# Nineteen small loads into unused columns, between the last weight loads of a decode layer

## The chip, the cores and the metric

The kernel runs on one core of one Trainium2 chip. A core has engines that run their own instruction streams: TensorE (PE, with its weight loads as PEld), VectorE (DVE), ScalarE (ACT), GpSimd (POOL) and SyncE (SP). They wait for each other by semaphores. Sixteen DMA engines move data between HBM and the on-chip memory (SBUF), and SP, ACT and POOL can issue loads to them. The metric is the device time of one execution in microseconds (us), lower is better.

## The reference

One decode step of a transformer layer with adaptive layer norm: four sequences (B = 4), one token each, width 512.

```
mod = (silu(c) @ w_mod) split in six: sa, ca, ga, sb, cb, gb
h = layernorm(x) * (1 + ca) + sa
x = x + ga * attention(h)      # 32 query heads on 8 kv heads of 128, the last 2048 cached positions, then @ wo
h = layernorm(x) * (1 + cb) + sb
x = x + gb * ((silu(h @ w1) * (h @ w3)) @ w2)     # w1, w3: 512 x 1792, w2: 1792 x 512
```

Everything is float32. The weights and the cached keys and values are about 101 MB, and each is read once.

## The kernel before

All large inputs come through one SBUF buffer, `ring`, of 6 x 8192 float32 columns on 128 partitions, cut into three slots of 16384 columns. A slot holds one group's keys and values (8 MB) or weights. The loads are issued by SP in the order in which they are needed (only wq goes through ACT): w_mod_a, the key and value blocks of seven groups, wo_mod (a half of wo and the rest of w_mod), the last group's keys with more of wo, its values, the rest of wo, then w1, w3 and w2. A load is issued as soon as the last reader of the columns that it overwrites is done, so SP waits for PE most of the time, and the loads stand in line at the DMA engines for some 40 us.

`Program` records each operation with the tiles that it reads and writes, adds the waits that overlaps ask for, and emits the operations engine by engine in the order of the code. Every recorded operation is emitted by one line, L57. A load that anyone waits for has a semaphore of its own. `do.mark()` cuts the program in two parts: the first part's semaphores are cleared by GpSimd (L136) once PE, DVE, ACT and SP have all passed the mark, which PE does just before its products with the last piece of w2.

Around the change stand these steps. `project_out(3)` multiplies with the last part of wo_mod that lies in columns 6144 to 8191 of slot 0; `mod_columns` reads columns 8192 to 16383 of it. Then `group(G - 1, [4, 5])` is the attention of the last group. The load of w3 goes to the upper half of slot 0, and the load of w2 to the first 7168 columns of the lower half, in four pieces of 7, 4, 2 and 1 blocks of 512 columns (`W2_CUTS`), so that the products with w2 can begin before all of it is there. Columns 7168 to 8191 of slot 0 are used by nothing after `project_out(3)`. After the attention come the second norm, the products with w1 (gate), with w3 (up), the product of both into `hidT`, and the products with w2: the first 7 blocks into `part`, the other 7 into `y_ps`. Two DVE operations and one store of 32 KB end the program.

Of the kernel before, what the change touches and what calls it, by code (L numbers as in the profile page):

```python
# [8 lines left out]
B, D, HQ, G, SK, DH, W, FF = 4, 512, 32, 8, 8192, 128, 2048, 1792  # L9
# [5 lines left out]
NF = len(CHUNKS)  # L15
W2_CUTS = [0, 7, 11, 13, 14]
EPS = 1e-5
HALF = 8192
# [127 lines left out]
def block_kernel(nc, w_mod_a, wq, kv_in, wo_mod, last_k_wo, last_v, wo, w1, w3, w2, out):  # L146
# [5 lines left out]
    do = Program(nc)  # L152
# [8 lines left out]
    slots = [ring[:, n * 2 * HALF : (n + 1) * 2 * HALF] for n in range(3)]  # L161
# [10 lines left out]
    def load(dst, src, cuts=(0, 1), queue="sync"):  # L172
        step = src.shape[1] // cuts[-1]
        for lo, hi in zip(cuts[:-1], cuts[1:]):
            do(queue, "dma_start", dst[:, lo * step : hi * step], src[:, lo * step : hi * step])
        return dst[:, : src.shape[1]]
# [114 lines left out]
    for half in range(2):  # L291
        qp = s_ps[half]
        for k in range(4):
            for i in range(4):
                at = ((half * 4 + i) * 4 + k) * 512
# [26 lines left out]
    def heads_out(g):  # L322

        otp = bank()[:, : R * B]
        if g < G - 1:
            do("tensor", "matmul", otp, o_sum, pick, start=True, stop=True)
        else:
            for c in range(NC):
                do("tensor", "matmul", otp, work[:, c * P : (c + 1) * P], pick_c[:, c].rearrange("p r b -> p (r b)"), start=(c == 0), stop=(c == NC - 1))
        do("vector", "tensor_copy", oT[:, g].rearrange("p r b -> p (r b)"), otp)  # L330
# [60 lines left out]
    do("vector", "tensor_scalar_add", cb1, cb1, 1.0)  # L391
    group(G - 1, [4, 5])
    w3_t = load(slots[0][:, HALF:], w3)
    w2_t = load(slots[0][:, :HALF], w2, W2_CUTS)
    heads_out(G - 1)
    project_out(G - 2)
# [118 lines left out]
```

## Time and profile before

| what | value |
|---|---|
| median of 3 runs | 242.45 us (242.39 to 242.96) |
| span of the profiled execution, first to last instruction | 241.1 us |
| busy share of PE, DVE, ACT, POOL | 61%, 23%, 10%, 1% |
| moved by the DMA engines | 101.38 MB, 421 GB/s on average |
| w1, w3 and the four pieces of w2 issued by SP | at 181.64, 192.84, 193.21, 193.68, 194.18 and 194.67 us |
| store of the result issued | at 239.56 us |

The profiled execution's span is 1.35 us shorter than the median time of the runs. The profile gives each group of instructions as engine, line, operation, output<-input, shape, count and times; "SPq" is SP's own queue, and "us to landing" counts from the issue of a load to the last of its completion signals. In the strip of 40 digits each digit is the busy share of the 16 DMA engines in one fortieth of the window, in tenths.

### The profile page before, as it was taken

Reading aid. Unit: us, or ns where it says so; the run is one execution under the profiler, and the core shown is the slowest. Engines: PE = TensorE matmul, PEld = TensorE weight load, DVE = VectorE, ACT = ScalarE, POOL = GpSimd, SP = SyncE. Lnnn points to the kernel's source line nnn. Section 1 sums busy time; section 2 is a strip of 40 time slices with the busy share of each in tenths; the row PEclk is TensorE's granted clock in tenths of the full one; section 3 lists DMA queues with packets and bytes.
Section 4 is the critical chain, followed back from the end, with each engine's and each line's share of the span. In section 5 each row is a group of like instructions: output and inputs, shape, how many; then the busy total and the mean of one; then the engine's idle time right before and its main releaser. Section 6 shows DMA issues by size and latency. Waiting matters only on the chain.

```text
span 241.1 us, 2468 instructions
## 1 busy us (share of the span) xinstructions
PE 146.8 (61%) x1103; PEld 52.8 (22%) x1103; DVE 55.2 (23%) x140; ACT 24.0 (10%) x36; POOL 2.6 (1%) x11
## 2 busy tenths in 40 slices
PE   0000169756782972945767586567296919964876
PEld 0000132213222312201311222221131202422333
DVE  4000220240303124123132124130312014103120
ACT  2000000103003003001200300300300000320100
POOL 3000000000000000000000000000000000000000
PEclk9999997995977799779797589797977997996899
DMA  8999989898989898989999999999999999999993
GB/s 316 414 436 425 500 370 500 351 511 359 511 359 503 370 502 370 489 383 478 391 479 391 478 394 468 402 468 405 457 413 424 435 405 435 407 432 426 416 415 133
DMA packets 2889, 101.38 MB, mean 421 GB/s; under 512 B 448, under 2 KB 448, under 8 KB 704
## 3 DMA queue, kind: packets, MB, share of 16 engines
q1 hardware_dynamic: 2736, 92.85, 89.5%
q10 hardware_dynamic: 144, 8.39, 8.1%
q8 instruction: 8, 0.13, 0.2%
q14 instruction: 1, 0.01, 0.0%
HBM read 101.20 MB, written 0.03 MB: 420 GB/s over the span
## 4 chain that ended last, share of the span: by engine, by line
DMA 73%; PE 20%; DVE 3%; ACT 2%; issue 0%; SPq 0%
DMA ring<-kv_in 30%; DMA ring<-wo_mod 17%; DMA ring<-w 15%; DMA ring<-w_mod_a 11%; PE s_ps L57 8%; PE bank L57 7%; PE o_ps L57 4%; PE a_ps L57 2%; ACT p_sb L57 2%; DVE nm L57 2%; DVE p_sb L57 0%; DVE e L57 0%; DVE sq L57 0%; DVE xc L57 0%; DVE tot L57 0%
## 5 line engine op out<-in xcount | busy, mean ns | idle before, releaser
L57 PE MATMUL s_ps<-ring,qT 128*32 128x512 f32 x256 | 37.0, 731 | 20.2 <-DMA ring<-kv_in 14.7
L57 PE MATMUL bank<-ident,p_sb 128*128 128x128 f32 (+1 forms) x136 | 27.4, 350 | 30.8 <-ACT p_sb L57 30.7
L57 PE MATMUL o_ps<-ring,pT 128*16 128x512 f32 x256 | 37.8, 696 | 0.0
L57 PEld LDWEIGHTS bank<-ident,p_sb 128*128 128x128 f32 (+1 forms) x136 | 19.6, 177 | 51.9 <-ACT p_sb L57 31.7
L57 ACT ACTIVATE p_sb<-s_ps,nm 128x2048 f32<-128x2048 f32 (+1 forms) x11 | 16.5, 1501 | 143.2 <-DVE oT L57 105.2
L57 DVE TENSOR_REDUCE nm<-s_ps 128x1 f32<-128x2048 f32 x7 | 16.0, 2292 | 34.5 <-PE s_ps L57 34.5
L57 DVE COPY pT<-bank 128x64 f32<-128x64 f32 x32 | 7.2, 224 | 56.1 <-PE bank L57 56.1
L57 PEld LDWEIGHTS s_ps<-ring,qT 128*32 128x32 f32 x256 | 9.0, 131 | 47.5 <-issue 20.7
L57 PE MATMUL bank<-ident,xs 128*128 128x128 f32 x1 | 0.5, 473 | 27.8 <-POOL xs L57 27.8
L57 PE MATMUL s_ps<-ring,h2T 128*32 128x512 f32 (+1 forms) x64 | 9.1, 664 | 2.3 <-DMA ring<-w 2.3
L57 PE MATMUL a_ps<-ring,oT 128*4 128x512 f32 x64 | 9.1, 709 | 2.0 <-DMA ring<-wo_mod 2.0
L57 PE MATMUL s_ps<-ring,hT 128*32 128x512 f32 x64 | 8.8, 711 | 0.4 <-DVE hT L57 0.4
L57 PEld LDWEIGHTS o_ps<-ring,pT 128*16 128x16 f32 x256 | 5.4, 98 | 11.6 <-issue 9.2
L57 DVE SCALAR_TENSOR_TENSOR o_own<-o_ps,rl,own 128x512 f32<-128x512 f32 x7 | 5.3, 751 | 11.1 <-PE o_ps L57 11.1
L57 DVE TENSOR_REDUCE o_sum<-o_own 128x128 f32<-128x512 f32 x7 | 7.2, 1029 | 0.2
L57 PE MATMUL bank<-ring,sc 128*32 128x256 f32 (+1 forms) x64 | 7.2, 610 | 0.0
L57 PEld LDWEIGHTS bank<-ident,xs 128*128 128x128 f32 x1 | 0.2, 180 | 27.8 <-POOL xs L57 27.8
L57 DVE TENSOR_SCALAR e<-e 128x16 f32<-128x16 f32 x1 | 0.2, 174 | 23.8 <-ACT e L57 23.8
L57 DVE TENSOR_REDUCE mx<-s_ps 128x1 f32<-128x512 f32 x4 | 2.8, 691 | 7.6 <-PE s_ps L57 7.6
L57 DVE COPY qT<-bank 128x64 f32<-128x64 f32 x8 | 2.2, 277 | 9.8 <-PE bank L57 9.4
L57 PEld LDWEIGHTS s_ps<-ring,h2T 128*32 128x32 f32 x64 | 2.6, 129 | 7.4 <-issue 4.5
L57 PE MATMUL s_ps<-ring,hidT 128*32 128x64 f32 (+1 forms) x126 | 3.7, 262 | 0.3 <-DVE hidT L57 0.3
(93 smaller groups left out, 55.4 us busy)
## 6 DMA issues: line engine op xcount, KB each, us to landing
ring<-w SPq DMA_DIRECT2D x2, 3584.0 KB, 38.3
ring<-last_k_wo SPq DMA_DIRECT2D x1, 6144.0 KB, 30.5
ring<-last_v SPq DMA_DIRECT2D x1, 4096.0 KB, 39.9
ring<-w_mod_a SPq DMA_DIRECT2D x1, 2064.0 KB, 26.6
ring<-wo SPq DMA_DIRECT2D x1, 2048.0 KB, 43.4
ring<-w SPq DMA_DIRECT2D x1, 1792.0 KB, 40.9
ring<-w SPq DMA_DIRECT2D x1, 1024.0 KB, 42.9
ring<-w SPq DMA_DIRECT2D x1, 512.0 KB, 43.7
```

The source lines that it names most:

```text
L57: op = Op(engine, lambda: getattr(getattr(self.nc, engine), method)(*args, **kw), [])
```

## The change

Between the load of w3 and the load of w2 twenty operations are added; nothing is removed. Fifteen are loads by SP: load n (1 to 15) takes n rows of 4n columns, 16n bytes a row, out of w3, and writes them to the same rows of the unused columns. Four are loads by GpSimd of 2, 8, 3 and 8 rows of 2048, 2064, 2080 and 2096 bytes, out of w3 too. The last is a GpSimd memset of all 1024 unused columns on 128 partitions, which waits for all nineteen loads. Nothing reads these columns.

```
     w3_t = load(slots[0][:, HALF:], w3)
+    spare = slots[0][:, NF * D : HALF]
+    for n in range(1, 16):
+        at = 2 * n * (n - 1)
+        do("sync", "dma_start", spare[:n, at : at + 4 * n], w3[:n, at : at + 4 * n])
+    for lo, hi, step, m in ((32, 34, 1, 512), (0, 32, 4, 516), (40, 43, 1, 520), (64, 96, 4, 524)):
+        do("gpsimd", "dma_start", spare[lo:hi:step, 480 : 480 + m], w3[lo:hi:step, 480 : 480 + m])
+    do("gpsimd", "memset", spare, 0.0)
     w2_t = load(slots[0][:, :HALF], w2, W2_CUTS)
```

The order of instructions changes on two engines. On SP, between wo and the end, this stood before (`w` stands for w1, w3 and w2; the shape is rows x columns, and `x2` are w1 and w3):

```order
L57 DMA ring<-wo 128x4096
L57 DMA ring<-w 128x7168 x2
L57 DMA ring<-w 128x3584
L57 DMA ring<-w 128x2048
L57 DMA ring<-w 128x1024
L57 DMA ring<-w 128x512
L57 DMA out<-p_sb 128x64
```

and this stands there now, from the twelfth small load on:

```order
L57 DMA ring<-w 12x48
L57 DMA ring<-w 13x52
L57 DMA ring<-w 14x56
L57 DMA ring<-w 15x60
L57 DMA ring<-w 128x3584
L57 DMA ring<-w 128x2048
L57 DMA ring<-w 128x1024
L57 DMA ring<-w 128x512
```

The four pieces of w2 have moved behind fifteen more issues on SP; none of the fifteen has a wait of its own, since the wait of w3 already covers it.

On POOL, which had nothing between the copy of x near the start and the clearing of the semaphores (`L136 ISA`), the difference is this:

```order
 L57 MEMSET xs 128x128
 L57 COPY xs<-ring 128x16
+L57 DMA ring<-w 2x512
+L57 DMA ring<-w 8x516
+L57 DMA ring<-w 3x520
+L57 DMA ring<-w 8x524
+L57 MEMSET ring 128x1024
 L136 ISA
```

The first of the four loads waits for PE (the last product of `project_out(3)`), the memset for nineteen loads, and the clearing now stands behind both. PE, DVE and ACT keep their instructions in the same order.

## The prediction

> **What bounds the kernel.** I read the page's head and its strip of DMA shares first, then the chain that ended last.
>
> ```profile
> span 241.1 us, 2468 instructions
> DMA  8999989898989898989999999999999999999993
> DMA packets 2889, 101.38 MB, mean 421 GB/s; under 512 B 448, under 2 KB 448, under 8 KB 704
> q8 instruction: 8, 0.13, 0.2%
> DMA 73%; PE 20%; DVE 3%; ACT 2%; issue 0%; SPq 0%
> ```
>
> The sixteen DMA engines are at 80 to 90% and more in every slice but the last, and 73% of the chain is waiting for loads. The kernel is bound by bytes; the end is set by the last ones, and the chain's last pieces show how:
>
> ```profile
> 192.84 37.00 DMA ring<-w
> 229.84 0.04 issue
> 229.88 3.71 PE s_ps L57 x20
> ...
> 234.91 0.27 DVE hidT L57
> 235.18 0.04 issue
> 235.22 3.80 PE s_ps L57 x138
> 239.02 0.02 issue
> 239.05 0.23 DVE p_sb L57
> ```
>
> The load of w3, issued at 192.84, lands at 229.84; hidT is ready at 235.18; then PE multiplies with w2 until 239.02. The chain books those 3.80 us to PE, so I looked at whether PE waits for w2 inside them. The issues of the four pieces, one row each of SP's timeline, their landings in the same order (KB each, us from issue to landing), and the stored result:
>
> ```profile
> 193.21 0.43 SPq L57 DMA_DIRECT2D ring<-w  x1
> 193.68 0.45 SPq L57 DMA_DIRECT2D ring<-w  x1
> 194.18 0.45 SPq L57 DMA_DIRECT2D ring<-w  x1
> 194.67 0.44 SPq L57 DMA_DIRECT2D ring<-w  x1
> ...
> ring<-w SPq DMA_DIRECT2D x1, 1792.0 KB, 40.9
> ring<-w SPq DMA_DIRECT2D x1, 1024.0 KB, 42.9
> ring<-w SPq DMA_DIRECT2D x1, 512.0 KB, 43.7
> ring<-w SPq DMA_DIRECT2D x1, 256.0 KB, 43.8
> out<-p_sb SPq DMA_DIRECT2D x1, 32.0 KB, 1.5
> ...
> 236.66 0.16 PEld L57 LDWEIGHTS s_ps<-ring,hidT 128*32 128x32 f32 x5 [0.43 <-DMA ring<-w]
> ```
>
> Sums: the pieces land at 234.1, 236.6, 237.9 and 238.5. The first is there 1.1 us before hidT asks for it. The second is waited for: PE's weight loads stand 0.43 us and go on at 236.66. The fourth lands 0.5 us before PE is done. So a delay of the last three pieces by d moves the end by d; a delay of the first by less than 1.1 us costs nothing by itself.
>
> The engines do not finish together, which decides who may be delayed. Busy time and DMA share (the last two columns are share and GB/s) in three stretches of the end, and the two queues in the window 230 to 238.6:
>
> ```profile
> 230.00:236.40 6.40, 5.86 (x51) 2.31 (x52) 0.91 (x3) 0.58 (x1) 0.00 (x0) 1.00 0.96 399
> 236.40:237.90 1.50, 1.50 (x74) 1.09 (x72) 0.00 (x0) 0.59 (x1) 0.00 (x0) 1.00 0.50 190
> 237.90:238.60 0.70, 0.70 (x62) 0.70 (x56) 0.00 (x0) 0.00 (x0) 0.00 (x0) 1.00 0.01 3
> ...
> q1 hardware_dynamic: 517, 2.82, 79.5%
> q8 instruction: 1, 0.02, 0.8%
> ```
>
> From 236.4 to 237.9 half of the engine time is used: about eight engines have finished, and eight carry on for some 1.5 us. A cause is in the second queue: one instruction fetch packet costs 0.8% of 16 engines x 8.6 us = 1.1 us on the one engine that it falls on, and the page counts eight of them. Which engines are the late ones no view says.
>
> **The change, part by part.**
>
> *Fifteen loads by SP: their issue.* SP's rows above stand 0.47 to 0.50 us apart, so fifteen more take 15 x 0.49 = 7.4 us, and w2's pieces are issued from 200.6 to 202.1. Cover: the engines are on w1 and w3 until w3 lands at 229.84, so there are about 27 us to spare, and an issue would have to take over 2 us each before the engines run dry. No row of SP shows a dearer issue than 0.45 us; I cost it at nothing.
>
> *Their packets.* They lie in the queue after w3 and before w2, hence they delay all four pieces of w2 and not w3. For the price I take the store, 128 rows of 256 bytes, in the window 240.3 to 240.8:
>
> ```profile
> DMA packets 144, 0.03 MB, mean 66 GB/s; under 512 B 144, under 2 KB 144, under 8 KB 144
> q1 hardware_dynamic: 144, 0.03, 31.1%
> ```
>
> 144 packets are 128 rows and 16 completions, one for each engine. They took 31.1% of 16 x 0.5 us = 2.49 us, or 17 ns each. The fifteen loads have 1 + 2 + ... + 15 = 120 rows of 16 to 240 bytes. The large loads spread eight rows to an engine; a load of n rows can use at most n engines. If the rows start from the same engine each time, the first engine gets one row and one completion of each load, 30 packets x 17 ns = 0.52 us, and the last gets none. Spread evenly it would be at most (120 + 240)/16 = 22.5 packets = 0.39 us; all rows on one engine, 135 packets = 2.3 us. I take 0.52, since a row to an engine is what the large loads show, and because the end goes by the latest engine.
>
> The Trainium skill, in "DMA: Bandwidth & Descriptors", section "Why a DMA increments its semaphore by 16 and not by 1", says that a load from SP uses the largest number of engines up to 16 that divides its outer size, and then the lowest-numbered ones. By that, n rows go to engines 0 to n-1, and the sum is the same 0.52 us on engine 0. No load in the trace of before has fewer than 128 rows, so no row bears on it.
>
> *What a load costs beside its packets, in a queue that is full.* The trace has 512 KB in 237.9 - 236.6 = 1.3 us and 256 KB in 238.5 - 237.9 = 0.6 us: half the bytes, half the time, so a further load costs between nothing and about 0.1 us (the landings are given to 0.1). For fifteen that is 0 to 1.5 us. I take 0, which the 1024 KB in 2.5 us support, and keep 1.5 for the range.
>
> The Trainium skill's same page, section "Anatomy of one DMA — SWDGE (gpsimd) path", gives a fixed part of about 2.0 us a DMA, and its "Rules for kernel authors" call a transfer under 64 KB mostly overhead. Nineteen in a row would be 38 us by it, an estimate. The pieces of w2 disagree as long as other loads are in line, with 0.6 us for 256 KB.
>
> *Four loads by GpSimd.* They wait for the last of `project_out(3)`; the products ran here:
>
> ```profile
> 183.60 5.31 PE L57 MATMUL a_ps<-ring,oT 128*4 128x512 f32 x32 [1.99 <-DMA ring<-wo_mod]
> 2.01 0.95 POOL L57 MEMSET qT<- 128x1024 f32 x1
> 27.50 0.21 POOL L57 COPY xs<-ring 128x16 f32<-128x16 f32 x1 [24.39 <-DMA ring<-w_mod_a]
> 233.62 0.43 DVE L57 COPY p_sb<-s_ps 32x256 f32<-32x256 f32 x1 [4.05 <-PE s_ps L57]
> ```
>
> So they are issued from 188.9 on, by a POOL that has been idle since 27.7. Before has no issue by POOL; SP's 0.45 is the nearest row, and with 28 us until w2's turn several us each would still be hidden. Their bytes come on top of a full queue wherever they land: 21 rows of 2 KB. w2's fourth piece has 8 such rows on each engine in 0.6 us, or 0.08 each. An engine gets one or two rows (21/16 = 1.3), 0.16, and up to four completions, 4 x 17 ns = 0.07: 0.23 us. On one engine alone it would be 21 x 0.08 = 1.7 us; nothing at all if they fall on early engines.
>
> *The memset.* It waits for the fifteen loads behind w3, so it starts about 230.5 and takes the 0.95 us of qT's row, of the same shape; nineteen waits may add 1 us. DVE stands idle for 4.05 us before 233.62, PE does not wait for POOL, and ring's columns there are read by nobody. Behind it on POOL is only the clearing, which PE's mark lets go shortly before 238.5: 6 us of cover. Without it the end would wait for POOL from about 241 on. Nothing.
>
> *Sum.* 0.52 + 0.23 = 0.75 us on the latest engine, if it is among those that take the most small rows. The span goes from 241.1 to 241.85. The median of the runs is 1.35 us above that span, and I leave this as it is: 242.45 + 0.75 = 243.2.
>
> **The rivals.**
>
> *Hidden by the early engines.* If the engines with most of the small rows are among the eight that finish 1.5 us early, they have room for 0.75 us. The late ones then bear, say, seven loads of the fifteen (14 x 17 ns = 0.24) and the GpSimd part (0 to 0.23): 0.25 to 0.5 us, 242.7 to 242.95. For it: the stretch with half of the engines done. Against it: eight of sixteen are late, so that all of the first few are early is the smaller part, and rows this short may cost more than the store's 17 ns. It ends inside 0.3% (0.73 us, up to 243.18), which is about what a measurement of this kernel can tell from no change.
>
> *One engine takes whole loads.* Were all rows of a small load on one engine, and that the same one, 135 packets x 17 ns = 2.3 us there; with GpSimd's 0.23 that gives 245.0, or 243.5 if the engine is an early one with 1.5 us of room. It decides from 0.75 us on the last engine. Against it: the large loads are spread.
>
> *Every small load makes its own round trip.* The store needs 1.5 us from issue to landing. If an engine finished each small load before it turned to the next, 15 x 1.5 = 22 us would stand between w3 and w2: 265. Against it: w2's 0.6 us for 256 KB.
>
> *A gain.* Were the instruction fetches shifted to other engines by the added traffic, the late half could end up to half of 1.5 us sooner: 242.45 - 0.75 = 241.7. Nothing in the change points there; it only could.
>
> **How the numbers follow.** Forecast (0.73 to 1.9 us more, the sum with the fixed part of up to 0.1 a load partly real): 0.45. Hidden or nearly: 0.42. One engine with whole loads: 0.07. Round trips, or a POOL so slow that it sets the end: 0.03. A gain over 0.3%: 0.03. Slower is 0.45 + 0.07 + 0.03 = 0.55, within 0.3% 0.42, faster 0.03. For the range I leave out the lower part of the hidden case, under 242.5 (about 0.05, with the 0.03 of a gain), and above 244.7 (0.75 + 1.5 from the unknown fixed part) most of the whole-load case and the round trips, about 0.1. The forecast's own range is 243.2 to 244.3.
>
> **What would show it.** In the profile of after: w2's pieces issued 7.4 us later with w3 landing within 0.3 us of 229.84; the four pieces landing later by the same 0.5 to 0.9 us each and PE's wait before the second piece longer by that; hidT no later than 0.3 us; the memset done by 233; the 1.5 us stretch with half of the engines still there. If w2's landings stay within 0.3 us, the early engines have hidden it; a first piece later than 1.1 us and with a gap of DMA share after 229.8 would mean round trips; landings later by 2 us with only one engine busy, whole loads on one engine. The prediction is wrong outright if SP's issues take over 2 us each, if w3 itself moves by over 0.5 us, or if the time outside the span changes because of loads from GpSimd.

## The result, and the profile after

The changed kernel takes 243.75 us (median of 4 runs, 243.72 to 243.83) where the kernel before takes 242.45: 1.3 us more, ratio 1.005 with a 95% interval of 1.0034 to 1.0066. The forecast was 0.75 us more (243.2) within 242.5 to 244.7. The profiled execution grew by the same amount, from 241.1 to 242.4, so the time lies inside the span. The page of after, from its head, its DMA queues and its chain:

```profile
span 242.4 us, 2497 instructions
DMA packets 3257, 101.44 MB, mean 419 GB/s; under 512 B 795, under 2 KB 795, under 8 KB 1072
q1 hardware_dynamic: 2976, 92.87, 89.5%
q0 software_dynamic: 128, 0.04, 0.1%
DMA 74%; PE 17%; DVE 3%; SPq 2%; ACT 2%; issue 1%
```

Bytes and the share of the main queue are as before; 240 packets are new on q1 (120 rows and 120 completions) and 128 on q0, the queue of GpSimd's loads. The last pieces of the chain that ended last, and the weight loads of PE that wait:

```profile
196.98 0.39 SPq L57
197.37 0.04 issue
197.41 40.51 DMA ring<-w
237.92 0.04 issue
237.96 2.34 PE s_ps L57 x128
240.30 0.02 issue
240.32 0.23 DVE p_sb L57
...
237.96 0.94 PEld L57 LDWEIGHTS s_ps<-ring,hidT 128*32 128x32 f32 x64 [1.40 <-DMA ring<-w]
```

Before, the chain went through hidT and booked the end to PE; now it names the second piece of w2, and PE's wait for it has grown from 0.43 to 1.40 us. The issues of w2's pieces in SP's timeline, and their landings (KB each, us from issue):

```profile
196.98 0.39 SPq L57 DMA_DIRECT2D ring<-w  x1
197.41 2.26 SPq L57 DMA_DIRECT2D ring<-w  x1
199.72 6.11 SPq L57 DMA_DIRECT2D ring<-w  x1
205.87 6.46 SPq L57 DMA_DIRECT2D ring<-w  x1
...
ring<-w SPq DMA_DIRECT2D x1, 1792.0 KB, 38.4
ring<-w SPq DMA_DIRECT2D x1, 1024.0 KB, 40.5
ring<-w SPq DMA_DIRECT2D x1, 512.0 KB, 39.4
ring<-w SPq DMA_DIRECT2D x1, 256.0 KB, 33.9
```

Sums: 235.4, 237.9, 239.1 and 239.8, against 234.1, 236.6, 237.9 and 238.5. All four pieces are 1.2 to 1.3 us later, while w3 (issued at 191.27, 38.8 us to landing) came at 230.1 instead of 229.8. So about 0.2 us arise ahead of w3's landing (the completions show them already at w1's, 221.51 against 221.32) and 1.1 between it and w2's first piece. Two stretches of the end (the last two columns are DMA share and GB/s) show that the engines are still out of step, but that fewer are done early:

```profile
230.00:236.40 6.40, 5.64 (x48) 2.35 (x51) 1.63 (x6) 0.58 (x1) 0.95 (x1) 1.00 0.98 397
236.40:237.90 1.50, 1.08 (x10) 0.15 (x3) 0.00 (x0) 0.38 (x1) 0.00 (x0) 1.00 0.83 336
```

The share from 236.4 to 237.9 rose from 0.50 to 0.83. The rest is as forecast: POOL's four issues and its memset are out of everybody's way:

```profile
187.69 2.18 POOL L57 DMA_DIRECT2D ring<-w  x4 [159.94 <-PE bank L57]
231.93 0.95 POOL L57 MEMSET ring<- 128x1024 f32 x1 [42.06 <-DMA ring<-w]
233.82 0.43 DVE L57 COPY p_sb<-s_ps 32x256 f32<-32x256 f32 x1 [3.03 <-PE s_ps L57]
235.11 0.25 DVE L57 TENSOR_TENSOR hidT<-eg,bank 128x56 f32<-128x56 f32 x1 [0.55 <-PE bank L57]
```

hidT is ready at 235.36, as w2's first piece lands: of the 1.1 us between the two nothing is left.

The completion signals recorded in the trace tell more than the views. Here are those of four small loads of the changed kernel (us; one value for each engine that reports, in order of time):

```
rows  completions
  1   192.12  228.61
  2   192.46  228.54 228.79
  5   193.41  228.45 228.92 229.07 229.33 229.63
  6   193.74  228.65 229.10 229.25 229.51 229.82 230.04
w3 (16 engines)          228.27 to 228.52 on eight, 229.26 to 230.04 on eight
w2, first piece          232.66 to 235.42
```

A load of n rows has one early signal at its issue and n later ones: n engines, one row on each. That is what the Trainium skill states in "DMA: Bandwidth & Descriptors", section "Why a DMA increments its semaphore by 16 and not by 1" (the lowest-numbered engines up to the largest divisor, the issuer writes the rest at once), and the trace agrees in both (it counts the engines and shows the same ones coming back, but does not number them). The engine that serves the one-row load reports at 228.61, then 228.79, and so on: 0.17 to 0.2 us from one small load to the next, although the packets were worked out at 17 ns each. The engine that the six-row load adds comes last, at 230.04, because it is one of the eight late ones.

### The profile page after: what moved, and what is told of

Same layout as the page of the kernel before. It is cut to its first block, busy times and chain, and to the rows that moved or that the text cites. A ratio compares the mean times of both kernels' runs of the same rounds, so it can differ in the third digit from the quotient of the medians.

```text
span 242.4 us, 2497 instructions
## 1 busy us (share of the span) xinstructions
PE 150.1 (62%) x1103; PEld 53.4 (22%) x1103; DVE 55.2 (23%) x140; ACT 24.0 (10%) x36; POOL 5.8 (2%) x16
## 4 chain that ended last, share of the span: by engine, by line
DMA 74%; PE 17%; DVE 3%; SPq 2%; ACT 2%; issue 1%
DMA ring<-kv_in 31%; DMA ring<-w 17%; DMA ring<-wo_mod 16%; DMA ring<-w_mod_a 11%; PE bank L57 7%; PE s_ps L57 5%; PE o_ps L57 4%; SPq L57 2%; DVE nm L57 2%; ACT p_sb L57 2%; PE a_ps L57 1%; DVE p_sb L57 0%; DVE e L57 0%; DVE sq L57 0%; DVE xc L57 0%
## 5 line engine op out<-in xcount | busy, mean ns | idle before, releaser
L57 PE MATMUL s_ps<-ring,qT 128*32 128x512 f32 x256 | 37.7, 743 | 19.6 <-DMA ring<-kv_in 12.4
L57 PE MATMUL bank<-ident,p_sb 128*128 128x128 f32 (+1 forms) x136 | 28.7, 361 | 30.8 <-ACT p_sb L57 30.7
L57 PE MATMUL o_ps<-ring,pT 128*16 128x512 f32 x256 | 38.7, 711 | 0.0
L57 PEld LDWEIGHTS bank<-ident,p_sb 128*128 128x128 f32 (+1 forms) x136 | 20.7, 184 | 52.8 <-ACT p_sb L57 31.7
L57 PE MATMUL s_ps<-ring,h2T 128*32 128x512 f32 (+1 forms) x64 | 9.7, 701 | 0.9 <-DMA ring<-w 0.6
L57 PE MATMUL s_ps<-ring,hT 128*32 128x512 f32 x64 | 9.8, 783 | 0.4 <-DVE hT L57 0.4
L57 PE MATMUL a_ps<-ring,oT 128*4 128x512 f32 x64 | 7.4, 592 | 1.1 <-DMA ring<-wo_mod 1.1
L57 POOL DMA_DIRECT2D ring<-w x4 | 2.2, 552 | 159.9 <-PE bank L57 159.9
## 6 DMA issues: line engine op xcount, KB each, us to landing
ring<-w SPq DMA_DIRECT2D x2, 3584.0 KB, 38.8
```

The costliest lines, as they stand in the source:

```text
L57: op = Op(engine, lambda: getattr(getattr(self.nc, engine), method)(*args, **kw), [])
```

## The experiments

Two theories stood against each other at the start, with a third for GpSimd's loads. **A, packets** (the prediction's): a small load costs an engine its row and its completion, 2 x 17 ns. **B, a price for each load**: 0.13 us on every engine that it uses, whatever it carries. The figure of B is from after: the late engine that takes ten of the fifteen loads (six rows and up) ends them at 231.88 and w2's first piece at 235.42; it ended w3 at about 229.8, so the first piece was due 4.3 us later, at 234.1, and is 1.3 us late (4.3 us is what lies between the two in the kernel before, 229.84 to 234.1). Each kernel was timed in turn with the kernel before, which ran at 242.42 to 242.49 us. The first two cuts of code below show what is gone against the changed kernel, the others what stands in place of the nineteen loads; the lines that set `spare` and the loops over n are in part left out, and the memset stays in every kernel that has small loads.

### The fifteen alone, and the four alone

```
-    for lo, hi, step, m in ((32, 34, 1, 512), ...):
-        do("gpsimd", "dma_start", spare[lo:hi:step, ...], ...)
```

> The fifteen loads of 1 to 15 rows by SP and the memset, without the four loads by GpSimd. Theory A (packets: 17 ns for each row and each completion, the prediction's): at most 0.52 us later than before, w2's last piece lands by 239.0. Theory B (each small load costs every engine that it uses about 0.13 us, whatever its rows carry): the latest engine takes ten or more of them, +1.1 to +1.3 us, w2's last piece lands at 239.6 to 239.8. Theory C (the GpSimd loads make the difference): 0 to +0.3 us.

Measured: 243.27 us against 242.42, ratio 1.004 (1.0027 to 1.0053), +0.85 us.

```
-    for n in range(1, 16):
-        at = 2 * n * (n - 1)
-        do("sync", "dma_start", spare[:n, at : at + 4 * n], w3[:n, at : at + 4 * n])
```

> The four loads by GpSimd and the memset, without the fifteen by SP. Theory A: up to +0.23 us. Theory B: 0 to +0.3 us, the landing of w3 later by that and the pieces of w2 unchanged behind it. Theory C: +1.0 us or more.

Measured: 242.59 us against 242.42, ratio 1.0008 (0.9999 to 1.0017), +0.17 us, which the interval does not tell from nothing. C is out: the time comes from SP's fifteen loads. They cost more than A's 0.52: the interval is 0.65 to 1.28 us, and B's lower end, 1.1, lies in it. w2's last piece landed at 239.4, later than A's 239.0 and earlier than B's 239.6 to 239.8. The two parts sum to 1.0 of the 1.3 us; the 0.3 left is inside the intervals.

### One engine alone: 24 loads of one row, 15 loads of three rows

```
+    for n in range(24):
+        do("sync", "dma_start", spare[:1, 40 * n : 40 * n + 32], w3[:1, 40 * n : 40 * n + 32])
```

> Instead of the nineteen loads, twenty-four loads by SP of one row of 128 bytes each, and the memset; all on one engine, one of those that finish w3 about 1.6 us before the last. Theory A: 48 packets x 17 ns = 0.8 us, less than the engine's room: no change. Theory B: 24 x 0.13 = 3.1 us on that engine, less 1.6 of room: +1.3 to +1.7 us, with one engine's landings of w2 alone behind the others'.

Measured: 244.09 us against 242.42, ratio 1.0072 (1.006 to 1.0085), +1.67 us. A, which expected no change, is out, and by 24 rows that are 3 KB together. The pieces of w2 in this kernel:

```profile
207.91 30.41 DMA ring<-w
...
ring<-w SPq DMA_DIRECT2D x1, 1792.0 KB, 29.1
236.40:237.90 1.50, 1.50 (x14) 0.30 (x6) 0.00 (x0) 0.00 (x0) 0.00 (x0) 1.00 0.52 206
```

Of the sixteen completions of the first piece fifteen come from 232.17 to 234.10 as before, and one at 235.86. That engine ended w3 early, at about 228.0, so its first piece was due 4.3 us later, at 232.3. It is 3.56 us late, 0.15 for each load.

The counterpart puts a like burden on early engines without exceeding their room:

```
+        do("sync", "dma_start", spare[:3, at : at + 4 * n], w3[:3, at : at + 4 * n])
```

> Instead of the nineteen loads, fifteen loads by SP of 3 rows each, and the memset: the three lowest engines take 15 of them, and in the run with 1 to 15 rows these three were among the eight that finish w3 about 1.5 us early. Theory A: 30 x 17 ns = 0.5 us, hidden: no change. Theory B: 15 x 0.13 to 0.15 = 2.0 to 2.2 us, less the room of 1.5 to 1.6: +0.3 to +0.7 us, with three engines' landings of w2 behind the others'.

Measured: 242.67 us against 242.49, ratio 1.0007 (0.9998 to 1.0016): not told from no change. This is below what B expected, but the trace shows the mechanism B names. The stretch of the end in this kernel:

```profile
236.40:237.90 1.50, 1.50 (x66) 0.82 (x62) 0.00 (x0) 0.53 (x1) 0.00 (x0) 1.00 0.70 279
```

The DMA share in it is 0.70, not 0.50: 3 of 16 engines more are busy (0.50 + 3/16 = 0.69). Five engines end the first piece before 233.0 where eight did. The three delayed ones have merged with the late half. The room of the early engines is real, and it swallowed 15 loads on each of three engines.

### All engines alike: 16 rows, then rows of 2 KB

```
+        do("sync", "dma_start", spare[:16, at : at + 4 * n], w3[:16, at : at + 4 * n])
```

> Instead of the nineteen loads, fifteen loads by SP of 16 rows each (16 to 240 bytes a row), and the memset: every engine gets one row of every load, the late ones too. Theory A: 30 packets x 17 ns = +0.52 us. Theory B: 15 x 0.13 = +1.95 us on all engines alike.

Measured: 245.0 us against 242.42, ratio 1.0102 (1.0089 to 1.0116), +2.58 us. w3 landed at 193.03 + 36.9 = 229.9 and the first piece of w2 at 236.2:

```profile
193.03 0.33 SPq L57 DMA_DIRECT2D ring<-w  x1
ring<-w SPq DMA_DIRECT2D x1, 3584.0 KB, 36.9
...
200.34 35.85 DMA ring<-w
236.20 0.14 issue
236.33 5.37 PE s_ps L57 x135
...
236.20:239.70 3.50, 3.37 (x18) 1.03 (x20) 0.00 (x0) 0.00 (x0) 0.00 (x0) 0.51 0.78 318
239.70:241.70 2.00, 1.96 (x129) 1.80 (x123) 0.00 (x0) 0.59 (x1) 0.00 (x0) 1.00 0.07 23
```

Of 6.25 us between the two, 4.3 are usual: 1.95 us for fifteen loads, 0.13 each, as B said to the tenth. The other 0.5 us is not in the loads. The first piece now comes after hidT is ready, PE starts late, and in this execution the granted clock was 0.51 from 236.2 to 239.7 (the column before the DMA share), where it was 1.0 at that place in the kernel before. PE ends 1.1 us after w2's last landing instead of 0.5. The kernel with rows of 2 KB, next, speaks for the clock and against the late first piece as the cause: there the piece comes later still, the granted clock is 1.0 from 237.8 to 241.4, and the end moves by no more than w2's landings (3.7 us). The clock was not changed by itself. The first piece's cover of 1.1 us, which the prediction named, is overdrawn here; in the changed kernel it was used up to the last tenth.

The same with 512 columns a row asks whether the 0.13 us runs beside a transfer:

```
+        p, at = n // 2 * 16, n % 2 * 512
+        do("sync", "dma_start", spare[p : p + 16, at : at + 512], w3[p : p + 16, at : at + 512])
```

> As the fifteen loads of 16 rows, but with rows of 2048 bytes: every engine gets 15 rows of 0.08 us. Theory A: 15 x (0.08 + 0.01) = +1.35 us, with a first piece of w2 0.3 us too late. Theory B1a (the 0.13 us runs beside the transfer, the longer of both counts): 15 x 0.13 = 1.95 us on the landings, +2.4 to +2.6 us in all, as with the short rows. Theory B1b (it comes on top of the transfer): 15 x 0.2 = 3.0 us on the landings, +3.5 us in all.

Measured: 246.18 us against 242.47, ratio 1.0153 (1.0139 to 1.0166), +3.71 us. The size is that of B1b (on top): the first piece landed at 200.3 + 37.5 = 237.8, 3.7 us late, 0.25 a load against 0.08 + 0.13. The trace does not show B1b's picture, though. The last nine of the fifteen loads completed 0.18 us apart (those ahead of them 0.22 to 0.30), just as the short ones of the kernel above, so their rows did run beside (B1a). What was dearer are the transfers themselves: the 240 rows took 0.13 us in the median instead of 0.08, eleven of w3's last packets took 1.2 to 1.9 us instead of 1.07, and w3 itself landed at 231.14, 1.3 us later than before. Each load writes all its rows into the same sixteen partitions from sixteen engines; whether that slows the transfers was not tried.

### Is it the row or the load: one load of 120 rows, one of 127

```
+    do("sync", "dma_start", spare[:120, :60], w3[:120, :60])
```

> Instead of the nineteen loads, one load by SP of 120 rows of 240 bytes, and the memset: as many rows as the fifteen loads have, on 15 engines, eight rows and one completion on each. Theory A: 9 x 17 ns = +0.15 us. Theory B1 (price of a load): 0.13 to 0.28 us. Theory B2 (price of a short row): 8 x 0.13 = +1.0 us.

Measured: 242.6 us against 242.47, ratio 1.0005 (0.9996 to 1.0013). As many rows as the fifteen loads have cost nothing that can be measured when they are one load. Rows are not the price.

```
+    do("sync", "dma_start", spare[:127, :60], w3[:127, :60])
```

> Instead of the nineteen loads, one load by SP of 127 rows of 240 bytes, and the memset. 127 has no divisor from 2 to 16, so all rows should lie on one engine, the early one with about 1.6 us of room, with a single completion. Theory A/packets: 127 x 18 ns = 2.3 us, less 1.6: +0.6 to +0.8 us. Theory B1 (0.13 us is the price of a load, or its completion): the same 2.3 us and one 0.13: +0.6 to +0.9 us. Theory B2 (0.13 us is the price of a short row): 16.5 - 1.6 = +15 us. If the rows are spread over all engines: no change.

Measured: 243.59 us against 242.47, ratio 1.0062 (1.0035 to 1.0089), with runs from 242.6 to 246.0. The size is near what was expected, and the reason is another. All rows are indeed on one engine, with one late completion, at 229.73; the engine had ended w3 at about 228.0, so 127 rows took 1.7 us, 14 ns each, and B2 is out. But SP was held up (the last line is the same stretch in the kernel before):

```profile
192.03 35.66 SPq L57 DMA_DIRECT2D ring<-w  x1
227.74 0.43 SPq L57 DMA_DIRECT2D ring<-w  x1
...
227.80:229.80 2.00, 0.92 (x8) 0.63 (x6) 1.08 (x4) 0.62 (x2) 0.00 (x0) 1.00 0.86 249
...
227.80:229.80 2.00, 0.51 (x4) 0.33 (x4) 0.92 (x4) 0.22 (x1) 0.00 (x0) 1.00 0.99 423
```

The issue of w2's first piece took 35.66 us instead of 0.43. It ended at 227.69; by the packet records the one engine began its 127 rows at 227.47 and ended them at 229.25 (its completion signals come some 0.5 us after the packets). So the piece seems to have been handed out only when that engine had worked some of its list off, and the others ran dry meanwhile (249 GB/s in the stretch from 227.8 to 229.8, where the kernel before has 423). A queue that is full for one engine then holds back the load for all sixteen. That the queue was full is inferred from these times; no view tells how much it holds.

```
+        do("sync", "dma_start", spare[:128, at : at + 4 * n], w3[:128, at : at + 4 * n])
```

> Fifteen loads of 128 rows (16 to 240 bytes a row) by SP, and the memset: eight rows and one completion on each engine for each load, 1920 rows in place of 240. Theory A: 15 x 9 x 15 ns = 2.0 us on the landings, +2.5 us in all. Theory B1a (the longer of 0.13 us and the packets): 2.0 to 2.2 us on the landings, as with one row an engine. Theory B1b (0.13 us on top of the packets): 3.7 us on the landings, +4.2 us in all. Theory B2 (each short row): 15 us.

Measured: 245.88 us against 242.47, ratio 1.0136 (1.0119 to 1.0153), +3.41 us, between the forms of B. The time cannot decide between them, because the same hold-up came in: with 1920 rows in line, SP issued w2's first piece only at 229.60, and in the stretch from 227.8 to 229.8 the engines moved 171 GB/s:

```profile
229.60 0.43 SPq L57 DMA_DIRECT2D ring<-w  x1
227.80:229.80 2.00, 0.57 (x4) 0.42 (x4) 1.01 (x4) 0.22 (x1) 0.00 (x0) 1.00 0.80 171
```

The completions do decide. The fifteen loads were done at 232.63, and with one row an engine, in the kernel with 16 rows, at 232.65; w3 landed at 229.85 and 229.95. Eight rows an engine cost no more than one: the longer of the two counts (B1a).

### Does the price hold with large transfers between

A control splits w2's first piece into its seven blocks; then seven small loads of 16 rows stand ahead of them, or one in front of each.

```
-    w2_t = load(slots[0][:, :HALF], w2, W2_CUTS)
+    w2_t = load(slots[0][:, :HALF], w2, [*range(8), *W2_CUTS[2:]])
```

> No small loads; the first piece of w2 is issued as seven loads of one block (256 KB) each. The control for the next two. Rows of 2 KB for rows of 14 KB cost 56 x 80 ns - 8 x 535 ns = 0.2 us on each engine, six more completions at 0.02 us 0.1 us: +0.2 to +0.4 us by every theory.

```
+    for n in range(7):
+        do("sync", "dma_start", spare[:16, 64 * n : 64 * n + 32], w3[:16, 64 * n : 64 * n + 32])
     (then the seven blocks)
```

> As the control, with seven loads of 16 rows of 128 bytes one after the other ahead of w2, and the memset. Theory A (packets): 14 x 17 ns = 0.24 us over the control. Theory B, both forms: 7 x 0.13 = 0.9 us over the control.

```
+    for n in range(7):
+        do("sync", "dma_start", spare[:16, 64 * n : 64 * n + 32], w3[:16, 64 * n : 64 * n + 32])
+        load(slots[0][:, n * D : n * D + D], w2[:, n * D : n * D + D])
```

> The same seven loads of 16 rows, but one in front of each of the seven blocks of w2, so that 0.64 us of transfer on each engine lies between two of them. Theory B-price (each small load costs an engine 0.13 us wherever it stands): 0.9 us over the control. Theory B-row (the price comes from short loads that follow each other, since a completion waits for the one before): 0 to 0.25 us over the control.

Measured, against 242.49: control 242.86 (ratio 1.0006 to 1.0023), seven in front 243.39 (1.0027 to 1.0052), one before each block 243.22 (1.0019 to 1.004). In front they cost 0.53 us over the control, between the theories. Interleaved they cost 0.36, but there the interval overlaps the control's, so this is not told from nothing. The last completions in the traces of the three:

```
                     w3      seventh block   between
control              229.88  234.64          4.76
seven in front       229.89  235.14          5.25
one before each      230.10  234.88          4.78
```

Measured from w3's end, the interleaved loads are free: a small load and the block behind it take 0.66 to 0.70 us together, and the block alone in the control 0.67 to 0.69. In the profiled execution 0.24 of the 0.3 us by which the interleaved kernel is longer were there before any small load: w1 landed at 221.56 instead of 221.32. The price belongs to short loads that follow each other.

The completions of the four trains also say why the price per load differed from run to run. For the engine that set w2's landing (us; "delay" is how much later w2's first piece or seventh block came after w3 than without the loads, "beside" the difference of the two columns before it):

```
                              loads   w3's end to       delay   beside   delay for
                                      last small load                    each load
seven in front                   7        1.31           0.49     0.82      0.07
changed kernel, late engine     10        2.08           1.32     0.76      0.13
16 rows                         15        2.70           1.95     0.75      0.13
one row                         24        4.34           3.56     0.78      0.15
```

Each short load takes 0.18 to 0.21 us of completion time, and of a whole train some 0.75 to 0.8 us run beside the transfer that follows it. So 0.13 is an average: each further load costs 0.18 us and more, and by these sums a train of up to four would be free, an estimate that no run tried.

The packet records show where the time is lost. In the kernel with 24 loads of one row, the rows and their completions all passed the engine between 227.5 and 227.9, a load every 15 ns, so the packets cost no more than the 2 x 17 ns that A put. The next packet on that engine, 14 KB of w2's first piece, took 3.27 us, and a later one 1.08; the other 126 packets of this piece took 0.53 to 0.55. With 16 rows 32 of the 128 packets took 0.9 to 2.0 us, in the changed kernel 17 took 0.8 to 1.8, and in the kernel before, in that with 120 rows in one load and in that with interleaved loads no packet of w2's first piece is drawn out like this. The transfer behind the train pays, while the completions of the train are worked off. (Long packets alone do not prove a train: the kernel with 127 rows, whose first piece was handed out late, has 20 of them.) What in the ending of a load takes the 0.18 us no run separates.

## Why the prediction was right, and where it was wrong

Direction and range held; the time came out 0.55 us above the value given. That the sum was no further off is in part luck: two of its errors had opposite signs. The range is not luck, since its upper part was kept for the term that failed.

- *What bounds the end.* Right. The delay went into all pieces of w2 alike, the end moved by as much, and PE's wait for the second piece grew by 0.97 us.
- *SP's issue.* Right as to cost: w2's first piece was issued 5.7 us after w3, not 7.8, and it was in line some 30 us before its turn. That the third and fourth piece were issued only at 199.72 and 205.87, because the issues before them took 2.26 and 6.11 us, was not foreseen. It was free here; with 127 rows on one engine it was not.
- *Their packets.* The price was high enough (14 ns a row in the load of 127, where 17 was taken), and where the rows lie was right.
- *What a load costs beside its packets.* This is the step that failed. It was taken as 0, with up to 0.1 us kept for the range, from w2's large pieces. The runs show 0.18 to 0.21 us on each engine for each short load that follows another, less some 0.75 us for the whole train: 1.3 us for ten loads, 1.95 for fifteen. Loads that keep an engine busy for 0.6 us and more do not show it, because the completion of one runs beside the transfer of the next; the only price list in the trace of before was of such loads.
- *The latest engine takes the most rows.* Wrong too, in the other direction. The three engines with the most small loads were early ones, and their room hid fifteen loads (three rows: no change that can be measured). What set the end was a late engine with ten loads: 10 x 0.13 = 1.3 us where the prediction put 15 x 2 x 17 ns = 0.52. One error took back part of the other.
- *GpSimd's loads and the memset.* The 0.23 us fits the +0.17 measured, but nothing at all would fit too (interval from 0 to 0.4). That w3 landed 0.2 us later does not decide it: in the kernels without GpSimd's loads it landed at 229.8 to 230.1 as well, but for the one with rows of 2 KB. The memset ended at 232.88, as forecast, in DVE's idle time.
- *The rivals.* The hidden case describes three rows, not the changed kernel. Whole loads on one engine and a round trip for each load did not occur: 1.5 us a load would have shown in every run.

The Trainium skill's fixed part of about 2.0 us a DMA ("DMA: Bandwidth & Descriptors", section "Anatomy of one DMA — SWDGE (gpsimd) path") does not add up in a queue: fifteen loads cost each engine 1.95 us together.

## What to carry to other kernels

In a stream of loads that bounds the end, count short loads by engine and not by bytes: one load of 120 rows was free, while a train of fifteen cost every engine that it used 1.95 us, 0.13 a load. One short load in front of each transfer of 0.64 us cost the landings nothing, so spreading such loads out is worth trying where they can't be merged. Look up which engines are behind (the DMA share of the last stretch tells how many), since a delay on the others is free until it reaches them. A load with few large divisors in its rows puts all of them on few engines, and if their queue fills, the issuer seems to stop for everybody.

## What was not expected of the hardware

- Completions of short loads on one engine follow each other by 0.17 to 0.21 us, though the loads' packets pass it in 15 ns, and the next large packet is drawn out instead: 3.27 us for one that usually takes 0.54.
- An issue by SP takes 0.3 to 0.45 us, but 2.26, 6.11 and 35.66 us were seen with many packets in line.
- GpSimd's four issues took 2.18 us together, and their loads of 4 to 16 KB left 128 packets on q0 for 21 rows.
